# Attention and two MLP layers on one core: a third load queue and a re-ordered start

## The chip, the cores and the metric

The kernel runs on one core of one Trainium2 chip. The metric is the device time of one execution in microseconds (us), the median of several runs; a part of the text speaks of one profiled execution, whose instructions were recorded. A change of under 0.2% (2.08 us) is about what a measurement of this kernel can't tell from no change.

## What is computed

```python
def _attn_ref(q, k, v, tau):                      # q, k, v: 1 x 6016 x 256
    qn = q / (norm(q, axis=1) + 1e-06)            # one norm per column, over all 6016 rows
    kn = k / (norm(k, axis=1) + 1e-06)
    s = kn.T @ qn / tau                           # 256 x 256
    a = softmax(s, axis=-1)
    return v @ a

x = v @ a                                         # 6016 x 256
x = gelu_sigmoid(x @ w_in) @ w_out                # hidden size 2048
x = leaky_relu(x @ w2_in) @ w2_out
```

The inputs are 32-bit floats (the weights come as 64-bit words that the kernel converts).

## The kernel before

**Front.** q and k are read once. A block is 128 rows of q and the same 128 rows of k, 256 KB together. `rows` (L327) says how many blocks each load tile has: six tiles of one, one of two, nine of four, then one of two and one of one, 47 blocks in all. Eight buffers hold tiles; `load_qk(j)` (L335) issues one transfer for q and one for k, from SyncE's queue (SP), except that the k of tiles 0 to 3 goes out from ScalarE's queue. `AHEAD = 8` tiles are issued before the loop, and each turn of the loop (L392) issues the tile eight further on, after the scores and squares of its own tile.

For each block TensorE adds 128 rows of k against 128 rows of q into two score banks (`scores`, L360). A 256-column product of plain 32-bit floats runs as two instructions, so a block costs four. From tile `LATE` on (15 blocks) only the first score half is done in the loop, and the second halves are kept as reserve work for later (`second_half`, L510). ScalarE squares q and k two blocks at a time and VectorE adds the squares into `acc`, which has two halves (one per block of the pair; `squares`, L352). When all tiles are through, L411 adds the second half of `acc` to the first, and `norms` (L372) sums the rows with four one-column products against `ones`, eight instructions in all. From their result VectorE and ScalarE make the inverse norms, then come the softmax halves (L457), and while these run TensorE transposes v and works off the reserve.

**Order of conversion work.** The weights are converted in the gaps of VectorE by a generator, `jobs` (L294): each `go_on(n)` lets the next n steps be issued. A piece of the first weight (`wi`) has five steps: a shift (L212), two word operations (L217, L221), a copy that is the high half (L240), and a subtraction that is the low half (through L99). Pieces of the second weight (`wo`) have the same three and then L233 and a subtraction. At the third step the next piece's load is issued on SP, and `scale_next` lets ScalarE scale the next piece (L182), unless the list `held` is filled.

**The step to the layers.** The softmax matrix is multiplied into `w_in` (`fold_products`, L485): `fold(f)` (L572) makes the weights of hidden part f from the converted piece wi of f, whose high half its first two products read and whose low half the next two. The first pair of row blocks goes through `hidden_first` (L746): for f = 0, each of two column halves u is multiplied, activated on ScalarE, split into high and low halves (`halves`, L94: ScalarE casts, VectorE subtracts) and then one conversion step is let through; for other f the split is done for both u at once with four conversion steps before the subtraction. All later products go through `terms` (L88):

```python
for w, x, start, stop in ((wh, ah, first, False), (wh, al, False, False), (wl, ah, False, last)):
```

Every product of 32-bit accuracy is thus three: high by high, high weight by low data, low weight by high data. Each engine executes its own queue strictly in the order written.

Of the kernel before, what the change touches and what calls it, by code (L numbers as in the profile page):

```python
# [17 lines left out]
def tile_kernel(  # L18
# [28 lines left out]
    nc = tc.nc  # L47
    _, N, C = q.shape
    F = w_out.shape[0]
    P = 128  # L50
    KC = C // P
    NF = F // P // 2
# [21 lines left out]
    ident = const.tile([P, P], F32, name="ident")  # L74

    def small(pool, n, name):
        return pool.tile([P, 32], F32, name=name)[:, :n]

    ones = const.tile([P, P], F32, name="ones")
# [5 lines left out]
    def bank(tag):  # L85
        return ps.tile([P, BLK], F32, tag=tag, name=tag)

    def terms(dst, ws, xs, first, last, more=False):  # L88

        (wh, wl), (ah, al) = ws, xs  # L90
        for w, x, start, stop in ((wh, ah, first, False), (wh, al, False, False), (wl, ah, False, last)):
            nc.tensor.matmul(dst, lhsT=w, rhs=x, start=start, stop=stop, skip_group_check=more)  # L92

    def halves(hi, lo, raw):  # L94
        nc.scalar.copy(hi, raw)  # L95
        nc.vector.tensor_tensor(out=lo, in0=raw, in1=hi.bitcast(F32), op=ALU.subtract)  # L96

    def add(out, in0, in1, op=ALU.add):
        nc.vector.tensor_tensor(out=out, in0=in0, in1=in1, op=op)  # L99

    def subtract(out, in0, in1):
        add(out, in0, in1, ALU.subtract)
# [11 lines left out]
    with tc.manual_schedule():  # L114
# [14 lines left out]
        etl = early.tile([P, KC, C], F32R, tag="tt", name="etl")  # L129

        nc.gpsimd.memset(ones, 1.0)
        make_identity(nc, ident)


        raws = {}
# [28 lines left out]
        def next_load():  # L164
            if to_load and len(raws) < 3:
                load_piece(to_load.pop(0))
# [12 lines left out]
        def scale_words(t):  # L179

            h = t[:, :, :, 1].bitcast(F32)
            nc.scalar.activation(out=h, in_=h, func=AF.Copy, scale=2.0 ** -112)  # L182
# [3 lines left out]
        held = [True]  # L186
# [6 lines left out]
        def scale_next():  # L193
            if held:
                return
            for key in to_convert[:2]:
                if key in raws and key not in scaled:
                    scale_words(raws[key])
                    scaled.add(key)
                    return  # L200
# [104 lines left out]
        def go_on(count):  # L305
            for _ in range(count):
                next(work, None)
# [3 lines left out]
        acc = front.tile([P, 2, 2, C], F32, name="acc")  # L311
# [4 lines left out]
        root, rr, rn = (small(front, 4, x) for x in ("root", "rr", "rn"))  # L316
# [7 lines left out]
        nc.vector.memset(acc, 0.0)  # L324


        rows = [1] * 6 + [2] + [4] * 9 + [2, 1]  # L327
        assert sum(rows) * P == N
        at = [sum(rows[:j]) * P for j in range(len(rows))]
        last = len(rows) - 1  # L330

        def qk(j):
            return big[(j // 2 + 2) % 4][:, j % 2]

        def load_qk(j):  # L335
            n = rows[j]
            for i, src in ((0, q), (1, k)):
                eng = nc.scalar if j < 4 and i == 1 else nc.sync
                eng.dma_start(  # L339
                    out=qk(j)[:, i, :n, :],  # L340
                    in_=src[at[j]:at[j] + n * P, :].rearrange("(p r) c -> p r c", r=n),
                )
# [1 line left out]


        AHEAD = 8
        V_TILE = 10
        LATE = last - 4
        s_ps = [bank("y00"), bank("y10")]
        nrm = bank("h0")  # L350

        def squares(j):  # L352
            t, n = qk(j), rows[j]
            for r in range(0, n, 2):
                m = min(2, n - r)
                sq = front.tile([P, 2, 2, C], F32, tag="sq", name="sq", bufs=3)[:, :, :m]
                nc.scalar.activation(out=sq, in_=t[:, :, r:r + m, :], func=AF.Square)  # L357
                add(acc[:, :, :m, :], acc[:, :, :m, :], sq)
# [12 lines left out]

        def norms():  # L372

            for i in range(2):
                for kc in range(KC):
                    nc.tensor.matmul(  # L376
                        nrm[:, 2 * i + kc:2 * i + kc + 1],
                        lhsT=acc[:, i, 0, kc * P:(kc + 1) * P],
                        rhs=ones[:, :1],
                        start=True,  # L380
                        stop=True,
                    )

        for j in range(AHEAD):
            load_qk(j)
            if j == 3:
                nc.scalar.preload_act_table(AF.Sqrt)

        warm = bank("h3")
        for _ in range(6):  # L390
            nc.tensor.matmul(warm[:, :P], lhsT=ones, rhs=ones, start=True, stop=True)
        for j in range(LATE + 1):  # L392
# [3 lines left out]
            if j + AHEAD <= last:  # L396
                load_qk(j + AHEAD)
            if j == V_TILE:
                next_load()
                nc.sync.dma_start(out=taub, in_=tau.partition_broadcast(P))  # L400
                for c in range(2):
                    nc.sync.dma_start(
                        out=qk(V_TILE)[:, c],
                        in_=v[c * BLK:(c + 1) * BLK, :].rearrange("(t p) c -> p t c", p=P),
# [3 lines left out]

        for j in range(LATE + 1, last + 1):
            squares(j)  # L410
        add(acc[:, :, 0, :], acc[:, :, 0, :], acc[:, :, 1, :])  # L411
        for j in range(LATE + 1, last + 1):
            scores(j, (0,))
        go_on(2)
        norms()

        nc.vector.reciprocal(out=rtau, in_=taub)
        nc.vector.tensor_scalar_add(rr, nrm[:, :4], 1e-35)
        nc.scalar.activation(out=root, in_=rr, func=AF.Sqrt)
        nc.vector.reciprocal(out=rn, in_=root)  # L420
        nc.vector.tensor_tensor(out=rr, in0=rr, in1=rn, op=ALU.mult)
# [22 lines left out]
        def transpose_v(kc, tags):  # L444
            for u, tag in enumerate(tags):
                vt[kc, u] = bank(tag)
                for i in range(BLK // P):
                    nc.tensor.transpose(  # L448
                        vt[kc, u][:, i * P:(i + 1) * P],
                        qk(V_TILE)[:, u, i, kc * P:(kc + 1) * P], ident,  # L450
                    )

        def split_v(kc, u):
            dst = xbt if kc else xa[0]
            halves(dst[:, 0, u], dst[:, 1, u], vt[kc, u])
# [39 lines left out]
        def fold_scale(raw, pw, kc):  # L495
            nc.scalar.activation(  # L496
                out=raw[:, 0::3] if kc == 0 else raw[:, 1:3],
                in_=pw.rearrange("p (s n) -> p s n", s=2), func=AF.Copy,
                scale=rden[:, kc:kc + 1],
            )  # L500
# [61 lines left out]
        fold_scale(raw0, pw0[1], 1)  # L562
        fold_half(raw0, 0, 1)
        nc.sync.dma_start(out=w1raw[0], in_=raw0)
        go_on(1)
        split_v(1, 1)
        nc.scalar.preload_act_table(AF.Gelu_apprx_sigmoid)
        first_products(0, [(0, 1), (1, 1)])
        held.clear()
        go_on(3)  # L570

        def fold(f):  # L572

            wi = ready.pop(f)
            pw = bank("h0" if f == 1 else "h3").rearrange("p (k n) -> p k n", k=KC)
            for kc in range(KC):
                fold_products(pw[:, kc], wi, kc)
            raw = early.tile([P, 4, P], F32, tag="tp", name="raw")
            for kc in range(KC):
                fold_scale(raw, pw[:, kc], kc)  # L580
            hi, lo = wa[f][:, 0, :4], wa[f][:, 1, :4]
            nc.vector.tensor_copy(hi, raw)
            subtract(lo, raw, hi.bitcast(F32))
            nc.sync.dma_start(out=w1raw[f], in_=raw)
# [161 lines left out]
        def hidden_first(f):  # L746

            s, g = f // NF, f % NF
            at = (A11, A12) if s == 0 else (A21, A22)
            h = late.tile([P, 2, BLK], F32, tag="cc", name="h")  # L750
            gd = late.tile([P, 2, 2, BLK], F32R, tag="gd", name="gd", bufs=2)
            for u in range(2):
                if g == 0:
                    hp = hp0[s, u]
                    first_products(1, [(s, u)])
                else:
                    hp = bank(f"h{2 * s + u}")
                    for kc, x in enumerate((xa[0], xbt)):
                        terms(hp, (wa[g][:, 0, at[kc]], wa[g][:, 1, at[kc]]),
                              (x[:, 0, u], x[:, 1, u]), kc == 0, kc == KC - 1)  # L760
                act(1, h[:, u], hp)
                if g == 0:
                    halves(gd[:, 0, u], gd[:, 1, u], h[:, u])
                    go_on(1)
            if g:
                nc.scalar.copy(gd[:, 0], h)
                if f < 2 * NF - 1:
                    go_on(4)
                subtract(gd[:, 1], h, gd[:, 0].bitcast(F32))
            for u in range(2):  # L770
                pend.append((1, 0, u, f, gd[:, 0, u], gd[:, 1, u]))
# [6 lines left out]
        for f in range(NF):  # L778
            for s in range(2):
                hidden_first(f + s * NF)  # L780

                if f + 1 < NF and s == 0 and f:
                    while f + 1 not in ready:
                        go_on(1)
                    fold(f + 1)
                if f == 0 and s == 0:
                    continue
                if f == 0:
                    while 1 not in ready:
                        go_on(1)  # L790
                    emit_y(1)
                    fold(1)
                    emit_y(3)
                    fetch()
                else:
                    emit_y(len(pend) - 2)
                if f + 1 < NF or s == 0:
                    go_on(2)
                fetch()
# [180 lines left out]
```

## Time and profile before

| | |
|---|---|
| median of 3 runs | 1040.09 us (1039.96 to 1041.32) |
| the profiled execution's own time | 1040.84 us |
| its span, first to last instruction | 1039.1 us |
| TensorE (PE) busy | 1029.1 us, 99% |
| VectorE (DVE) busy | 774.8 us, 75% |
| ScalarE (ACT) busy | 592.5 us, 57% |
| GpSimd (POOL) busy | 0.8 us |
| mean granted TensorE clock | 1.000 of full |

The profile names a group of instructions by line, engine, operation, and output <- inputs. In the timeline the columns are start, length, engine, line, operation, how many, and in brackets how long the engine had been idle before and what released it. Successive matmuls overlap, so the length of one is longer than the distance to the next. "PEld" is the weight load of TensorE, "SPq" and "ACTq" a queue's issue of transfers.

### The profile page before, as it was taken

The page shows a single profiled execution, that of the slowest core. Times are in us where ns is not written, and L with a number is a line of the kernel's source. Part 1 is how long each engine was busy: PE and PEld are TensorE (multiplying, and loading weights), DVE is VectorE, ACT ScalarE, POOL GpSimd, SP SyncE. Part 2 cuts the span into 40 slices and gives each one's busy share as a digit, 9 for nine tenths or more (in the row PEclk, how much of TensorE's full clock was granted, in tenths as well). Part 3 has the DMA queues.
Part 4 walks back from the last instruction along what each step waited for, and adds up shares of the span by engine and source line. Part 5 has one row for each costly group of instructions (what it writes and reads, how often), then busy time and mean ns, then how long its engine had stood idle before and what let it go on. Part 6 is the DMA issues. An engine that isn't in the chain of part 4 may idle for free.

```text
span 1039.1 us, 12654 instructions
## 1 busy us (share of the span) xinstructions
PE 1029.1 (99%) x4670; PEld 868.0 (84%) x4670; DVE 774.8 (75%) x1195; ACT 592.5 (57%) x880; POOL 0.8 (0%) x7
## 2 busy tenths in 40 slices
PE   8999999999999999999999999999999999999998
PEld 7878888888888888888998888888888888888997
DVE  6889968888888888888866667667577667676655
ACT  5665556565666666665656555555555555455453
POOL 0000000000000000000000000000000000000000
PEclk9999999999999999999999999999999999999999
DMA  8745324014224223222744002001200300300202
GB/s 327 270 132 145 119 82 94 18 31 122 81 72 124 79 71 120 79 95 104 258 168 152 1 1 46 37 1 22 60 0 10 72 1 1 77 1 1 41 1 36
DMA packets 120941, 81.82 MB, mean 79 GB/s; under 512 B 93488, under 2 KB 105520, under 8 KB 119600
## 3 DMA queue, kind: packets, MB, share of 16 engines
q1 hardware_dynamic: 116592, 80.04, 25.6%
q10 hardware_dynamic: 4288, 0.98, 0.4%
q8 instruction: 36, 0.59, 0.2%
q14 instruction: 25, 0.20, 0.1%
HBM read 55.05 MB, written 25.95 MB: 78 GB/s over the span
## 4 chain that ended last, share of the span: by engine, by line
PE 95%; DMA 2%; DVE 2%; ACT 1%; issue 0%; ACTq 0%; SPq 0%; DVEq 0%
PE y L92 49%; PE h L92 43%; DMA qk<-in_k_dram 2%; DVE acc L99 1%; PE h L491 1%; PE y L364 1%; ACT sq L357 0%; ACT cv L182 0%; DVE xb L96 0%; PE h L376 0%; PE h L448 0%; ACTq L339 0%; PE y L448 0%; ACT raw L496 0%; PE y L491 0%
## 5 line engine op out<-in xcount | busy, mean ns | idle before, releaser
L92 PE MATMUL y<-gd,wo 128*128 128x512 f32 (+1 forms) x1248 | 296.9, 386 | 0.1
L92 PE MATMUL h<-xa,wa 128*128 128x512 f32 (+1 forms) x1152 | 276.2, 385 | 0.2 <-ACT raw L496 0.2
L92 PEld LDWEIGHTS y<-gd,wo 128*128 128x128 f32 x1248 | 233.7, 188 | 44.7 <-DVE gd L96 0.5
L92 PEld LDWEIGHTS h<-xa,wa 128*128 128x128 f32 x1152 | 215.9, 188 | 40.7 <-ACT raw L496 0.7
L92 PE MATMUL y<-g,wo 128*128 128x512 f32 (+1 forms) x1044 | 246.8, 385 | 0.0
L92 PEld LDWEIGHTS y<-g,wo 128*128 128x128 f32 x1044 | 196.0, 188 | 36.3
L92 PE MATMUL h<-xb,wa 128*128 128x512 f32 (+1 forms) x888 | 217.2, 385 | 0.4 <-DVE xb L96 0.4
L92 PEld LDWEIGHTS h<-xb,wa 128*128 128x128 f32 x888 | 166.6, 188 | 31.9 <-DVE xb L96 0.8
L99 DVE TENSOR_TENSOR tv<-tp,h 128x512 f32<-128x512 f32 (+1 forms) x88 | 59.3, 674 | 113.2 <-PE h L92 108.1
L99 DVE TENSOR_TENSOR cc<-tv,h 128x512 f32<-128x512 f32 (+1 forms) x176 | 116.0, 673 | 35.7 <-PE h L92 35.3
L96 DVE TENSOR_TENSOR gd<-cc,gd 128x1024 fp32r<-128x1024 f32 (+1 forms) x87 | 104.0, 1196 | 0.0
L817 ACT COPY tp<-h 128x512 f32<-128x512 f32 (+1 forms) x87 | 50.4, 579 | 91.8 <-PE h L92 90.1
L95 ACT CAST gd<-cc 128x1024 fp32r<-128x1024 f32 (+1 forms) x87 | 90.0, 1034 | 0.0
L596 ACT ACTIVATE cc<-cc 128x1024 f32<-128x1024 f32 (+2 forms) x49 | 50.3, 1027 | 38.8 <-DVE cc L99 38.8
L596 ACT ACTIVATE tt<-tt 128x512 f32<-128x512 f32 (+1 forms) x48 | 30.0, 625 | 72.5 <-DVE tt L99 72.5
L99 DVE TENSOR_TENSOR tt<-tt,h 128x512 f32<-128x512 f32 (+1 forms) x88 | 59.5, 676 | 9.5 <-DVE tt L99 0.5
L99 DVE TENSOR_TENSOR tt<-tv,h 128x512 f32<-128x512 f32 (+1 forms) x88 | 59.5, 676 | 9.2
L594 ACT ACTIVATE cc<-cc 128x1024 f32<-128x1024 f32 (+1 forms) x40 | 41.6, 1040 | 41.2 <-DVE cc L99 41.2
L99 DVE TENSOR_TENSOR g<-tt,g 128x512 fp32r<-128x512 f32 (+1 forms) x87 | 58.5, 673 | 7.2 <-ACT g L828 7.0
L594 ACT ACTIVATE tt<-tt 128x512 f32<-128x512 f32 (+1 forms) x40 | 24.9, 623 | 62.4 <-DVE tt L99 62.4
L99 DVE TENSOR_TENSOR g<-tp,g 128x512 fp32r<-128x512 f32 (+1 forms) x87 | 58.6, 673 | 0.0
L841 ACT CAST g<-tp 128x512 fp32r<-128x512 f32 (+1 forms) x87 | 53.3, 612 | 2.8
(111 smaller groups left out, 705.6 us busy)
## 6 DMA issues: line engine op xcount, KB each, us to landing
cv<-in_moe_w_in_dram SPq DMA_DIRECT2D x32, 256.0 KB, 3.3
cv<-in_moe_w_out_dram SPq DMA_DIRECT2D x16, 512.0 KB, 3.7
wa<-w2a SPq DMA_DIRECT2D x8, 896.0 KB, 4.6
x<-stg SPq DMA_DIRECT2D x5, 1024.0 KB, 4.3
stg<-x SPq DMA_DIRECT2D x5, 1024.0 KB, 5.1
out_dram<-o SPq DMA_DIRECT2D x80, 64.0 KB, 1.9
qk<-in_q_dram SPq DMA_DIRECT2D x9, 512.0 KB, 10.2
qk<-in_k_dram SPq DMA_DIRECT2D x9, 512.0 KB, 10.7
```

The source lines that it names most:

```text
L92: nc.tensor.matmul(dst, lhsT=w, rhs=x, start=start, stop=stop, skip_group_check=more)
L95: nc.scalar.copy(hi, raw)
L96: nc.vector.tensor_tensor(out=lo, in0=raw, in1=hi.bitcast(F32), op=ALU.subtract)
L99: nc.vector.tensor_tensor(out=out, in0=in0, in1=in1, op=op)
L364: nc.tensor.matmul(s_ps[h][:, :C], lhsT=t[:, 1, r, h * P:(h + 1) * P], rhs=t[:, 0, r, :], start=(j == 0 and r == 0), stop=(j == last and r ...
L491: nc.tensor.matmul(pw, lhsT=e[:, d, c0], rhs=wi[:, x, d], start=i == 0, stop=i == len(todo) - 1)
L594: nc.scalar.activation(out=out, in_=in_, func=AF.Gelu_apprx_sigmoid)
L596: nc.scalar.activation(out=out, in_=in_, func=AF.Prelu, alpha=0.01)
L817: nc.scalar.copy(tp, pa)
L841: nc.scalar.copy(g11[:, 0], tp)
```

## The change

The change does the following.

- **Load tiles.** `rows` becomes four tiles of one block, ten of four, one of two and one of one. The tiles 4 and 5 (four blocks each) are issued from GpSimd's queue, q and k both: four transfers of 512 KB. The k of tiles 0 to 3 stays on ScalarE's queue, all else on SP. `V_TILE`, the loop turn that loads v and the first weights, goes from 10 to 8. `make_identity`, GpSimd work, moves behind the first eight tiles' loads.
- **Norms.** The addition of the halves of `acc` goes. `norms` sums both halves by eight one-column products, the second half first, and a four-column addition on VectorE joins the two sums.
- **Products.** `terms` takes the low half of the data last, after the low half of the weight.
- **Conversion steps.** A `go_on(1)` ahead of `split_v(1, 1)` goes. `held` is cleared not ahead of the first hidden part but after its second column half. At f = 1 (first s) `held` is filled again, six steps are let through in place of four, and `held` is cleared after the `fold` that follows.

```diff
-        for w, x, start, stop in ((wh, ah, first, False), (wh, al, False, False), (wl, ah, False, last)):
+        for w, x, start, stop in ((wh, ah, first, False), (wl, ah, False, False), (wh, al, False, last)):
...
-        make_identity(nc, ident)
...
-        rows = [1] * 6 + [2] + [4] * 9 + [2, 1]
+        rows = [1] * 4 + [4] * 10 + [2, 1]
...
-                eng = nc.scalar if j < 4 and i == 1 else nc.sync
+                eng = nc.gpsimd if j in (4, 5) else nc.scalar if j < 4 and i == 1 else nc.sync
...
-        V_TILE = 10
+        V_TILE = 8
...
-            for i in range(2):
-                for kc in range(KC):
-                    nc.tensor.matmul(
-                        nrm[:, 2 * i + kc:2 * i + kc + 1],
-                        lhsT=acc[:, i, 0, kc * P:(kc + 1) * P],
+            for m in (1, 0):
+                for i in range(2):
+                    for kc in range(KC):
+                        col = 4 * m + 2 * i + kc
+                        nc.tensor.matmul(
+                            nrm[:, col:col + 1],
+                            lhsT=acc[:, i, m, kc * P:(kc + 1) * P],
...
         for j in range(AHEAD):
             load_qk(j)
             if j == 3:
                 nc.scalar.preload_act_table(AF.Sqrt)
+        make_identity(nc, ident)
...
-        add(acc[:, :, 0, :], acc[:, :, 0, :], acc[:, :, 1, :])
...
-        nc.vector.tensor_scalar_add(rr, nrm[:, :4], 1e-35)
+        nc.vector.tensor_scalar_add(rr, nrm[:, 4:8], 1e-35)
+        add(rr, rr, nrm[:, :4])
...
-        go_on(1)
         split_v(1, 1)
...
         first_products(0, [(0, 1), (1, 1)])
-        held.clear()
         go_on(3)
...
                     halves(gd[:, 0, u], gd[:, 1, u], h[:, u])
+                    if f == 0 and u == 1:
+                        held.clear()
+                        scale_next()
                     go_on(1)
...
-                if f < 2 * NF - 1:
+                if f == 1:
+                    held.append(True)
+                    go_on(6)
+                elif f < 2 * NF - 1:
                     go_on(4)
...
                     fold(f + 1)
+                    if held:
+                        held.clear()
+                        scale_next()
```

## Rows read from the trace of the kernel before

**Rows 1.** Busy time by stretch: us, each engine's busy (instructions), PEclk, DMA share, GB/s.

```profile
0.00:15.00 15.00, 10.97 (x46) 9.07 (x47) 6.29 (x8) 6.34 (x9) 0.84 (x7) 1.00 0.80 263
...
80.00:130.00 50.00, 50.00 (x245) 42.31 (x244) 46.62 (x76) 28.49 (x46) 0.00 (x0) 1.00 0.43 132
```

**Rows 2.** Timeline of TensorE, 9 to 28 us: the score products.

```profile
11.06 1.97 PE L364 MATMUL y<-qk 128*128 128x256 f32 x8 [1.28 <-DMA qk<-in_k_dram]
14.67 13.62 PE L364 MATMUL y<-qk 128*128 128x256 f32 x62 [1.64 <-DMA qk<-in_k_dram]
```

**Rows 3.** Timeline of SyncE's queue in short windows: issues of q.

```profile
0.73 1.83 SPq L339 DMA_DIRECT2D qk<-in_q_dram  x4
...
3.58 0.33 SPq L339 DMA_DIRECT2D qk<-in_q_dram  x1
...
6.88 0.43 SPq L339 DMA_DIRECT2D qk<-in_q_dram  x1
...
13.32 0.33 SPq L339 DMA_DIRECT2D qk<-in_q_dram  x1
```

**Rows 4.** Transfers issued from 0.7 and from 6.8 us: size, us to landing.

```profile
qk<-in_q_dram SPq DMA_DIRECT2D x1, 128.0 KB, 2.6
...
qk<-in_q_dram SPq DMA_DIRECT2D x1, 512.0 KB, 6.4
```

**Rows 5.** Busy time by stretch, 0 to 15 us: the last column is GB/s.

```profile
0.00:4.00 4.00, 3.01 (x13) 3.01 (x14) 0.91 (x1) 1.35 (x2) 0.84 (x7) 1.00 0.53 154
4.00:8.00 4.00, 3.89 (x17) 3.06 (x17) 2.58 (x4) 2.94 (x6) 0.00 (x0) 1.00 0.91 283
8.00:12.00 4.00, 2.72 (x14) 2.08 (x12) 1.57 (x3) 1.60 (x2) 0.00 (x0) 1.00 0.84 262
12.00:15.00 3.00, 1.36 (x7) 0.91 (x6) 1.23 (x1) 0.45 (x2) 0.00 (x0) 1.00 0.99 384
```

**Rows 6.** Timeline, 39 to 60 us: last scores, the added halves, the norms.

```profile
38.70 3.40 PE L364 MATMUL y<-qk 128*128 128x256 f32 x15
...
42.24 0.69 DVE L99 TENSOR_TENSOR acc<-acc 128x512 f32<-128x512 f32 x1
...
42.99 1.05 PE L376 MATMUL h<-ones,acc 128*128 128x1 f32 x8 [0.89 <-DVE acc L99]
```

**Rows 7.** Timeline of VectorE, 57 to 65 us: splits and conversion steps.

```profile
58.02 0.68 DVE L96 TENSOR_TENSOR xb<-y,xb 128x512 fp32r<-128x512 f32 x1
...
61.01 0.42 DVE L240 CAST wi<-ta 128x512 fp32r<-128x512 f32 x1
61.40 0.69 DVE L96 TENSOR_TENSOR gd<-h,gd 128x512 fp32r<-128x512 f32 x1
62.01 0.68 DVE L99 TENSOR_TENSOR wi<-ta,wi 128x512 fp32r<-128x512 f32 x1
63.47 0.69 DVE L96 TENSOR_TENSOR gd<-h,gd 128x512 fp32r<-128x512 f32 x1 [0.78 <-ACT gd L95]
```

**Rows 8.** Timeline of TensorE and ScalarE, 57 to 65 us: first hidden part, fold of f = 1.

```profile
58.76 2.10 PE L92 MATMUL h<-xb,wa 128*128 128x512 f32 x8 [0.36 <-DVE xb L96]
...
62.19 0.60 ACT L594 ACTIVATE h<-h 128x512 f32<-128x512 f32 x1 [0.82 <-DVE gd L96]
...
62.41 0.84 PE L491 MATMUL h<-wi,eth 128*128 128x256 f32 x4
...
64.05 1.32 PE L92 MATMUL y<-gd,wo 128*128 128x512 f32 x5
```

**Rows 9.** Timeline of TensorE and ScalarE, 72.3 to 75.7 us: after the fold of f = 2.

```profile
72.31 0.86 PE L92 MATMUL h<-xa,wa 128*128 128x512 f32 x3
73.00 0.85 PE L92 MATMUL h<-xb,wa 128*128 128x512 f32 x3
74.10 0.96 PE L92 MATMUL h<-xa,wa 128*128 128x512 f32 x3 [0.24 <-ACT raw L496]
...
72.66 0.68 ACT L182 ACTIVATE cv<-cv 128x512 f32<-128x512 f32 x1
```

More of the change, by code (lines that the diff above doesn't have):

```diff
@@ L372, in norms @@
         def norms():
-            for i in range(2):
-                for kc in range(KC):
-                    nc.tensor.matmul(
-                        nrm[:, 2 * i + kc:2 * i + kc + 1],
-                        lhsT=acc[:, i, 0, kc * P:(kc + 1) * P],
[L379 to L382, printed above, removed]
+            for m in (1, 0):
[5 more added lines that the diff above has]
+                            lhsT=acc[:, i, m, kc * P:(kc + 1) * P],
+                            rhs=ones[:, :1],
+                            start=True,
+                            stop=True,
+                        )
         for j in range(AHEAD):
```

## The prediction, made before the changed kernel ran

> **What bounds the kernel now.** The page comes first: TensorE is busy for 1029.1 of 1039.1 us, so whatever the change does elsewhere, the time moves only where TensorE waits or where it gets more to do. The busy time by stretch says where that is: in the first 15 us TensorE is busy for 10.97, and from 80 us on the stretch is full, 50.00 of 50.00, at the full clock [rows 1]; the later stretches look the same, up to the last output. So at most some 10 us are to be had, and those that this change touches lie before 80 us. I read that part in order of time, with the timeline.
>
> *Data.* After the six one-block tiles TensorE waits 1.28 us for the two-block tile and, when that is done, 1.64 us for the first tile of four [rows 2]: 2.92 us together. From 14.67 us on it never waits for q and k again; 62 matmuls in 13.62 us are 0.22 us each, 0.88 for a block.
>
> *Issue.* SP issues four q in its first 1.83 us, but the next only at 3.58 [rows 3]. The first q, out at 0.73, landed 2.6 us later, at 3.33 [rows 4]. In the same way the 512 KB out at 6.88 land 6.4 us later, at 13.28, and an issue follows at 13.32, with seven others out in between. So a transfer of SP and ScalarE goes out when the one eight before it is in: that, not SP's own work, holds the early loads back.
>
> *Rate.* Up to 12 us the DMA engines move 154, 283 and 262 GB/s, and 384 in the next 3 us [rows 5]. Summed up that is 0.62 MB by 4 us, 1.75 by 8, 2.80 by 12 and 3.95 by 15.
>
> *Norms.* TensorE's scores end at 42.10 (38.70 + 3.40), VectorE's last square is added when the addition of the halves begins, at 42.24, and TensorE waits 0.89 us for that addition before the norms [rows 6].
>
> *Conversions.* From 57 to 75 us there are small waits: for the low half of xb, for that of wi, for ScalarE's fold scaling [rows 7 to 9].
>
> **The change part by part.**
>
> *Load tiles.* Twelve blocks stood before TensorE's last wait was over in the old order: eight in the first seven tiles, four in the next. In the new order the same twelve are tiles 0 to 5, and 12 x 0.262 MB = 3.15 MB must be in before TensorE can run through. By the rates, 3.15 MB had moved at 12.92 us (12 + 0.35 / 0.384), and the tile was usable at 14.67, 1.75 us later. The GpSimd issues don't occur in this trace, so I bound them. Best: both waits go, -2.92 us. Worst: the bytes come at the old rate, but GpSimd's two tiles share the engines with tiles 6 and 7 from SP, which follow q 3 closely. At an equal share for half of that time 1.05 MB of the later tiles come in between, tile 5 needs 4.2 MB, which is 15.66 us by the rates and 17.4 with the same 1.75: +2.7 us. Between: as many bytes by the same time in the right order, so that TensorE has done eight blocks and gets the next four at 14.67 as now. I take that, **0**, because the rows show the engines moving data nearly without a break from 4 us on (share 0.91 and 0.84), and an earlier issue doesn't make bytes move faster by itself. Both ends stay for the range. The number of blocks before LATE (32), the 15 in the tail and the block after which v is loaded (24) are as before, so nothing changes behind. make_identity waits behind four issues on GpSimd; its result is first read by the transposes behind the norms, some 40 us later, so it costs nothing unless an issue hangs that long. SP's q of tile 6 moves up past the four transfers that left its queue.
>
> The skill has a rule that would make it come out otherwise. The Trainium skill, "DMA: Bandwidth & Descriptors", section "Queues, rings and completion order", says that each DMA engine takes turns between the queues that have work for it, a packet at a time. No row here shows three queues at once; by that rule the load term is the +2.7 of the worst case and not 0, and it is the mechanism of the first rival.
>
> *Norms.* Four more one-column products are eight more instructions, 1.05 us by the row of the present eight. The second half of acc is complete one addition before the end, so they can begin when the scores end, 42.10, and run to 43.15; the first half's follow to 44.20. Now the norms end at 42.99 + 1.05 = 44.04 [rows 6]. So **+0.16**: a wait of 0.89 is filled with 1.05 of work. VectorE's 0.69 goes, but it isn't what ends last any more. The extra four-column addition lies under transposes and reserve scores, where TensorE has work of its own; if that cover went it would cost one short operation.
>
> *Low data last.* The number of products is the same and each loads its weights as before; from 80 us on TensorE doesn't wait, so nothing is won there: **0**. Before that it gives VectorE one product more for the low half of data and takes one from the low half of weights.
>
> *The step left out and held.* VectorE now splits xb 0.60 us earlier (the low half of wo steps behind it), and ScalarE does the scaling of a piece after both column halves of the first hidden part and not ahead of the first. That takes away the 0.36 that TensorE waits for xb [rows 8]. But every conversion step of this stretch now comes one place later, and the first that is late is the low half of wi for f = 1. Now the order on VectorE is high half of wi (61.01), gd of the second column half (61.40), low half of wi (62.01, done 62.69), and then an idle stretch until gd of the next part (63.47) [rows 7]. In the new order the high half of wi slides behind gd: gd starts 0.39 earlier, at 61.01. ScalarE's next activation, which waits for just that gd as h has one buffer [rows 8], starts at 61.80 in place of 62.19; the gd that hangs on it, 1.28 us after, at 63.08. The low half of wi now stands behind this gd, since one go_on(1) less has been spent: 0.61 later, at 63.69, done at 64.37 and not at 62.69. The fold's third product reads it. TensorE began the fold at 62.41 and went on to 64.05 [rows 8], with the low half as its bound in both cases, so the fold ends 64.37 - 62.69 = **+1.68** later, and what was gained for xb only makes TensorE wait longer there. Behind TensorE's fold stand 18 products that are ready; they wait with it. A VectorE that overtakes (if the wait for ScalarE is shorter than now) would bring this down to 0.
>
> *Held at f = 1.* The matmuls that follow the fold of f = 2 need the bank that ScalarE's fold scaling empties, and ScalarE first scales a weight piece for 0.68. Without it TensorE would go on one step (73.00 - 72.31 = 0.69) after 73.00, at 73.69, not 74.10 [rows 9]: **-0.41**. Six steps in place of four fill a stretch in which VectorE waits for ScalarE, and bring it back to its old place in the conversions.
>
> Sum: 0 + 0.16 + 0 + 1.68 - 0.41 = +1.43 us. On the profiled execution's 1040.84 (a span of 1039.1 and 1.7 around it) that is 1042.27; that execution was 0.75 above the median, and on the median it is 1041.5.
>
> **The rivals.**
>
> *Slower: the queues take turns.* Tile 5 comes after half of tiles 6 and 7, at 17.4 us. For it: SP's queue has tile 6 ready to go at 3.33, when the first q is in, long before 2 MB can have moved. Against it: GpSimd begins earlier, and its descriptors may be ahead in each engine. The price is +2.7 on top, 1040.09 + 1.43 + 2.7 = 1044.2. A milder form is that one-block tiles 1 to 3 wait behind GpSimd's 4 KB rows. It decides for slower as soon as tile 5 is usable after 15.3 us (2.08 - 1.43 = 0.65 after 14.67).
>
> *Faster: the data waits go.* If more transfers under way lift the rate of the first 12 us to the 384 GB/s seen behind, tiles 4 and 5 come before TensorE wants them, -2.92. For it: the low rate goes with the time in which transfers are held back. Against it: the engines' share is already 0.8 to 0.9 there. With 0.16 - 0.41, and the fold's wait at 0 to 1.68, it is -3.2 to -1.5, or 1036.9 to 1038.6.
>
> *The low half of wi isn't late* and the data come as now: 0.16 - 0.41 = -0.25, 1039.8. It needs VectorE to reach it before gd, against the written order.
>
> *The third queue isn't one:* if GpSimd's transfers are counted among the same eight, they leave at 3.33 or later, as tiles 4 and 5 do now. The load term is then the 0 of the forecast.
>
> **How the numbers follow.** The forecast (with the last rival inside) has 0.34, turns between queues 0.32, the data waits gone 0.24, wi in time 0.10. The likeliest gives 1041.5, own range 1040.0 to 1042.6. Faster by over 0.2% (under 1038.0; about what a measurement of this kernel tells from no change) is most of the third: 0.22. Slower by over 0.2% (above 1042.2) is the second and the forecast's upper edge: 0.34. Within 0.2%: 0.44. The range goes from between the ends of the fast rival, 1037.3, to the slow one's 1044.2.
>
> **What would show it.** Right: TensorE's last wait for q and k ends near 14.7 us; no wait between the scores and the norms, which take 2.1 us; the fold of f = 1 waits for the low half of wi for over a microsecond; no wait after the fold of f = 2. Wrong: a rate above 350 GB/s before 10 us (the fast rival), a landing of tile 5 beyond 15.3 us or a late tile 1 (the slow one), or a wi low half that is done before the second gd.

## The result and the profile after

The changed kernel takes 1046.78 us in the median of 5 runs (1044.94 to 1047.67), the kernel before 1040.33 beside it: a ratio of 1.006 with a 95% interval of 1.0048 to 1.0072. It is slower, and by more than the range allowed (1044.2). The profiled execution was the fastest of the five, 1044.94 us with a span of 1043.0.

TensorE's last product starts at 1037.19 us and not at 1033.88, so of the 4.10 us between the two profiled executions +3.31 lie ahead of it. From its start to the end of the span it is 5.8 us and not 5.2: the change and the four kernels below with both its tiles and GpSimd's queue all have 5.8, the others 5.2 to 5.5, and why isn't shown. The medians differ by 2.35 us more than the profiled executions, and that part stands in no trace. I divide the 3.31 at two marks: the end of the scores, and the start of the transposes of v behind the norms. The scores end at 44.51 in place of 42.10 (+2.41); from there to the transposes it is 1.54 us in place of 1.80 (-0.26); from there to the last product 991.14 in place of 989.98 (+1.16).

TensorE's timeline of the changed kernel, from the first scores to the transposes of v. The waits of [rows 2] and [rows 6] are answered by these lines:

```profile
3.73 2.19 PE L363 MATMUL y<-qk 128*128 128x256 f32 x8
8.68 1.13 PE L363 MATMUL y<-qk 128*128 128x256 f32 x4 [2.76 <-DMA qk<-in_k_dram]
11.04 5.19 PE L363 MATMUL y<-qk 128*128 128x256 f32 x15 [1.23 <-DMA qk<-in_k_dram]
...
41.76 2.75 PE L363 MATMUL y<-qk 128*128 128x256 f32 x12
44.34 1.84 PE L377 MATMUL h<-ones,acc 128*128 128x1 f32 x16
46.05 1.07 PE L450 MATMUL h<-ident,qk 128*128 128x128 f32 x8
```

After two tiles TensorE waits 2.76 us for tile 2 and then 1.23 for tile 3, both tiles of one block. It never waits for tiles 4 and 5. The products behind the second wait are slow: 15 in 5.19 us, where 62 took 13.62 before. The busy time by stretch tells why; the columns are those of [rows 5], with PEclk, the granted clock, third from the end:

```profile
6.00:8.00 2.00, 0.00 (x0) 0.00 (x0) 0.09 (x1) 0.00 (x0) 0.00 (x0) 1.00 1.02 366
8.00:10.00 2.00, 1.13 (x4) 0.68 (x4) 0.68 (x1) 0.63 (x1) 0.00 (x0) 1.00 1.05 410
10.00:12.00 2.00, 0.96 (x3) 0.78 (x4) 0.28 (x2) 0.93 (x2) 0.00 (x0) 0.79 1.03 421
12.00:14.00 2.00, 2.00 (x6) 1.64 (x5) 1.65 (x2) 1.60 (x2) 0.00 (x0) 0.50 1.02 414
14.00:16.00 2.00, 2.00 (x9) 1.67 (x9) 1.89 (x2) 1.88 (x2) 0.00 (x0) 0.86 1.03 414
```

After those two waits the granted clock is 0.50, the 1.2 GHz level, and six products stand in 2 us, where stretches at the full 2.4 GHz have eleven (keep_busy below shows two). From 6 us on the engines move 366 to 421 GB/s, more than the 283 and 262 of before [rows 5]. So bytes came faster, and the wrong ones came first. The transfers by queue, from 4 to 6 and from 6 to 8 us (q0 is GpSimd's queue, q1 SP's, q10 ScalarE's; packets, MB, share of the engines' time):

```profile
q0 software_dynamic: 128, 0.46, 58.0%
q1 hardware_dynamic: 64, 0.07, 17.4%
q10 hardware_dynamic: 31, 0.03, 6.6%
...
q0 software_dynamic: 123, 0.47, 61.8%
q10 hardware_dynamic: 142, 0.13, 20.6%
q1 hardware_dynamic: 143, 0.13, 20.0%
```

From 6 to 8 us the three queues have nearly the same number of packets, but GpSimd's are 4 KB and the others 1 KB: 0.47 MB go to tiles that nobody wants yet and 0.26 to the two that TensorE waits for. From 4 to 6 us it is more uneven, 0.46 MB against 0.10, and GpSimd's queue has more packets than the other two together. Equal turns don't explain that stretch, and no run here does. The q of tile 3, issued in the window from 2.1 us, needs 7.8 us to land; its like needed 4.3 before (the second line, the median of two):

```profile
qk<-in_q_dram SPq DMA_DIRECT2D x1, 128.0 KB, 7.8
...
qk<-in_q_dram SPq DMA_DIRECT2D x2, 128.0 KB, 4.3
```

Behind the norms, VectorE's steps that answer to [rows 7], and then TensorE's products that answer to [rows 8] and [rows 9], both from the timeline of the changed kernel:

```profile
63.05 0.69 DVE L96 TENSOR_TENSOR gd<-h,gd 128x512 fp32r<-128x512 f32 x1
63.65 0.42 DVE L239 CAST wi<-ta 128x512 fp32r<-128x512 f32 x1
65.11 0.69 DVE L96 TENSOR_TENSOR gd<-h,gd 128x512 fp32r<-128x512 f32 x1 [1.04 <-ACT gd L95]
65.72 0.69 DVE L99 TENSOR_TENSOR wi<-ta,wi 128x512 fp32r<-128x512 f32 x1
```

```profile
64.12 0.50 PE L493 MATMUL h<-wi,eth 128*128 128x256 f32 x2 [0.27 <-DVE wi L239]
66.46 0.50 PE L493 MATMUL h<-wi,eth 128*128 128x256 f32 x2 [1.83 <-DVE wi L99]
...
67.75 4.27 PE L92 MATMUL y<-gd,wo 128*128 128x512 f32 x18
...
77.41 0.85 PE L92 MATMUL h<-xa,wa 128*128 128x512 f32 x3
```

VectorE stands idle for 1.04 us until ScalarE has the next gd, with the low half of wi in its queue behind it, and TensorE waits 1.83 us for that half. The products behind the fold start at 67.75, and those that had waited for ScalarE's scaling [rows 9] at 77.41, now without a wait.

The five runs differ with the clock: mean granted 0.998 and 0.997 at 1044.94 and 1045.64 us, 0.994 at 1046.78, 1047.51 and 1047.67. Only the first was recorded instruction by instruction.

### The profile page after: what moved, and what is told of

Its sections match the earlier page's. It is cut to its first block, busy times and chain, and to the rows that moved or that the text cites. A ratio compares the mean times of both kernels' runs of the same rounds, so it can differ in the third digit from the quotient of the medians.

```text
span 1043.0 us, 12673 instructions
## 1 busy us (share of the span) xinstructions
PE 1030.6 (99%) x4678; PEld 870.2 (83%) x4678; DVE 774.6 (74%) x1194; ACT 593.8 (57%) x879; POOL 3.2 (0%) x11
## 4 chain that ended last, share of the span: by engine, by line
PE 97%; DMA 1%; DVE 0%; ACT 0%; ACTq 0%; issue 0%; SPq 0%
PE y L92 49%; PE h L92 43%; PE y L363 4%; DMA qk<-in_k_dram 1%; PE h L493 1%; DMA cv<-in_moe_w_in_dram 0%; DVE gd L96 0%; ACT h L594 0%; PE h L377 0%; PE y L493 0%; ACTq L338 0%; ACT L568 0%; ACT gd L95 0%; PE h L450 0%; PE y L450 0%; DVE wo L99 0%
## 5 line engine op out<-in xcount | busy, mean ns | idle before, releaser
L594 ACT ACTIVATE cc<-cc 128x1024 f32<-128x1024 f32 (+1 forms) x40 | 41.7, 1042 | 42.4 <-DVE cc L99 42.4
```

What stands on the lines that cost most here:

```text
L594: nc.scalar.activation(out=out, in_=in_, func=AF.Gelu_apprx_sigmoid)
```

## The experiments

Medians, with the kernel before run on the same chip; the last column is the range of the mean granted clock over a kernel's runs. The kernel before had 0.997 to 1.000 itself, with runs from 1039.19 to 1043.01 us. My theory was that GpSimd's rows hold up the one-block tiles, that the waits for these bring the clock down, and that the fold's wait comes from VectorE's order; the rivals stand with each expectation.

| kernel | us | before beside it | ratio, 95% interval | clock |
|---|---|---|---|---|
| the change | 1046.78 | 1040.33 | 1.0048 to 1.0072 | 0.994 to 0.998 |
| old_loads | 1042.77 | 1040.44 | 1.0008 to 1.003 | 0.996 to 1.000 |
| new_loads | 1043.52 | 1040.44 | 1.0016 to 1.0037 | 0.996 to 0.997 |
| keep_busy | 1043.62 | 1040.44 | 1.0022 to 1.0041 | 0.997 to 0.999 |
| fold_early | 1044.7 | 1040.44 | 1.002 to 1.0046 | 0.995 to 0.997 |
| sp_only | 1039.79 | 1040.0 | 0.9986 to 1.0006 | 0.998 to 1.000 |
| pool_small | 1038.52 | 1040.0 | 0.9979 to 0.9998 | 0.998 to 1.000 |
| both_mended | 1042.26 | 1040.0 | 1.0011 to 1.0029 | 0.999 to 1.000 |
| old_loads_fold | 1039.9 | 1040.0 | 0.9991 to 1.001 | 0.998 to 1.000 |
| small_all | 1038.24 | 1040.27 | 0.997 to 0.9988 | 0.999 to 1.000 |
| small_old_terms | 1037.96 | 1040.27 | 0.9968 to 0.9986 | 0.999 to 1.000 |

### The load tiles alone, and all but the load tiles

The first kernel is the change without its load tiles:

```diff
-        rows = [1] * 4 + [4] * 10 + [2, 1]
+        rows = [1] * 6 + [2] + [4] * 9 + [2, 1]
...
-                eng = nc.gpsimd if j in (4, 5) else nc.scalar if j < 4 and i == 1 else nc.sync
+                eng = nc.scalar if j < 4 and i == 1 else nc.sync
...
-        V_TILE = 8
+        V_TILE = 10
```

> The changed kernel with the load tiles of before (six tiles of one block, no transfer from GpSimd, v at turn 10); norms, product order and conversion steps stay changed. Theory (the third queue delays the one-block tiles, and the waits bring TensorE's clock down): no wait above 1.7 us for q and k, clock 1.000, norms about 0.2 us later than in the kernel before, the fold of f = 1 still some 1.6 late: 1041.3 to 1042, that is 1 to 1.5 us over before and 5 under the change. Rival (the loss comes from the norms and the conversion steps): still over 1044.

The second is the kernel before with these lines the other way round, and `make_identity` behind the loads.

> The kernel before with nothing but the new load tiles, GpSimd's queue, the moved identity and v at turn 8. Theory: tiles 2 and 3 usable near 8.7 and 11 us as in the changed kernel, clock below 1.000, scores done 2 to 5 us later: 1042.5 to 1045.5. Rival (the loads give time, the other parts lose it): 1040 or less.

The load tiles alone cost 3.1 us (1043.52 against 1040.44), all else 2.3, and 5.4 together against the 6.45 of the change. So the theory holds for the loads: their trace has the two waits again (1.64 and 1.47 us), the clock falls to 0.50 behind them, and the scores end at 46.24 (43.70 + 2.54):

```profile
12.00:14.00 2.00, 2.00 (x6) 1.55 (x6) 1.45 (x2) 2.00 (x3) 0.00 (x0) 0.50 1.01 406
14.00:16.00 2.00, 2.00 (x6) 1.58 (x5) 1.69 (x2) 0.45 (x2) 0.00 (x0) 0.50 1.04 416
...
43.70 2.54 PE L363 MATMUL y<-qk 128*128 128x256 f32 x11
```

The waits are shorter than in the change's profile, where TensorE came to the first of them sooner: the eight products ahead of it took 3.64 us here and 2.19 there. But the low clock lasts longer: what a wait costs isn't its length alone. Without the load tiles more was left than I had expected (1041.3 to 1042, at a clock of 1.000). The stretch from the transposes to the last product is 991.13 us there, as in the change; its recorded execution was among the fastest of its ten (1040.98), and the others ran at 0.996 to 1.000.

### TensorE kept at work in the two waits

```diff
+            for _ in range((0, 0, 10, 5)[j] if j < 4 else 0):
+                nc.tensor.matmul(warm[:, :P], lhsT=ones, rhs=ones, start=True, stop=True)
             scores(j, range(KC) if j < LATE else (0,))
```

> The changed kernel with 10 and 5 additional products of ones by ones (128 columns, no use of their result) ahead of the scores of tiles 2 and 3, where TensorE waits. Theory (the clock drops because TensorE stands idle there): granted clock 1.000 from 11 to 15 us, scores done 1 to 1.5 us sooner than in the changed kernel's profile, and all runs alike, 1043 to 1044. Rival (the clock falls for another reason): half clock after 11 us as before, and runs from 1045 to 1048.

The profile is as the theory has it: the data come nearly as late as in the change (ScalarE's first squares of tiles 2 and 3 start at 8.24 and 10.61 us, in the change at 8.66 and 11.07), but the clock stays at 1.00, eleven instructions go through in 2 us where there were six, and the scores end at 42.37 (37.67 + 4.70), 2.1 us sooner.

```profile
12.00:14.00 2.00, 2.00 (x11) 1.77 (x10) 1.68 (x2) 1.13 (x2) 0.00 (x0) 1.00 1.04 422
14.00:16.00 2.00, 2.00 (x11) 1.77 (x10) 1.08 (x2) 1.40 (x2) 0.00 (x0) 1.00 1.01 404
```

Of that, 0.46 is a tile 3 that landed sooner (its scores begin at 10.58 and not at 11.04). So the clock fell because TensorE stood idle there, and beside the waits themselves, 3.99 us, the low clock cost some 1.7. That all runs would be alike was a miss: they go from 1042.66 to 1045.2. One wait of 1.8 us was left in this kernel, that for wi.

### The low half of wi sooner

```diff
+                if f == NF and u == 0:
+                    go_on(1)
                 if g == 0:
                     halves(gd[:, 0, u], gd[:, 1, u], h[:, u])
...
-                    go_on(1)
+                    if f != NF or u:
+                        go_on(1)
```

> The changed kernel with one conversion step of the second hidden part moved ahead of the first split there, so that VectorE makes the low half of wi while it waits for ScalarE. Theory (the fold of f = 1 waits for that half): the wait of 1.83 us there falls below 0.4, and the time by 1.3 to 1.7 us against the change at the same clock. Rival (another wait takes its place): less than 0.5.

The wait for the low half is 0.22 in place of 1.83:

```profile
67.32 0.50 PE L493 MATMUL h<-wi,eth 128*128 128x256 f32 x2 [0.22 <-DVE wi L99]
```

From the transposes to the last product it is 989.56 us (48.52 to 1038.08), 1.58 less than in the change and 0.42 less than in the kernel before. The median is 2.1 below that of the change (measured in another set of runs, whose kernel before is 0.1 higher), in spite of longer data waits in its recorded run (3.71 and 1.56 us). The step was the one foreseen, and no other wait took its place.

### Both mended

The two edits together: the data come late, but TensorE has no long wait.

> The changed kernel with the additional products ahead of tiles 2 and 3 and the conversion step moved ahead, so that TensorE has no wait of over 0.5 us left before 80 us. Theory (what differs from run to run is the clock after a wait; in the kernel with additional products alone the fold's wait was left): clock 0.999 or more in all runs, spread under 1 us, 1041 to 1042. Rival (the spread has another source): runs again from 1042 to 1045.

All ten runs lie from 1041.8 to 1042.61, with a clock of 0.999 or 1.000. One data wait of 0.95 us was left, and the median lies 0.3 us over what was expected. With the wait for wi (keep_busy) the runs spread over 2.5 us, without it over 0.8. That supports the clock as the source of the spread; at which place it fell in the runs that were not recorded isn't shown.

### Which part of the loads: the queue or the tile sizes

In sp_only the tiles are the change's, but no transfer goes through GpSimd; in pool_small the tiles are those of before, and GpSimd's queue has tiles 4 and 5, of one block. Both are otherwise the kernel before, with `make_identity` behind the loads.

```diff
# sp_only
-        rows = [1] * 6 + [2] + [4] * 9 + [2, 1]
+        rows = [1] * 4 + [4] * 10 + [2, 1]
...
-        V_TILE = 10
+        V_TILE = 8
# pool_small
-                eng = nc.scalar if j < 4 and i == 1 else nc.sync
+                eng = nc.gpsimd if j in (4, 5) else nc.scalar if j < 4 and i == 1 else nc.sync
```

> The kernel before with the new load tiles (four of one block, ten of four, v at turn 8), all transfers but the first four k from SyncE's queue, none from GpSimd. Theory (GpSimd's 4 KB rows take turns with the 1 KB rows, packet for packet): tiles 2 and 3 land near 5 and 6.5 us as in the kernel before and TensorE does not wait for them; it waits once, some 3 us, for tile 4. Scores done about as before; 1040 to 1042.5. Rival (the larger tiles delay tiles 2 and 3, whatever queue they are on): waits for tile 2 and 3 as in the change, 1043 or more.

> The kernel before with its own tiles of one block, but tiles 4 and 5 (1 KB rows like tiles 0 to 3) from GpSimd's queue, and the identity moved. Theory (rows of one size share fairly, and four more transfers under way lift the rate): the one-block tiles land without a wait, over 330 GB/s before 10 us, the waits for q and k fall from 2.9 to under 1.5 us, norms 1 to 2.5 us sooner, clock 1.000: 1038 to 1039.5. Rival (GpSimd's queue itself is what delays): waits as in the change, over 1042.

TensorE's waits for q and k, first of sp_only and then of pool_small:

```profile
6.20 1.99 PE L363 MATMUL y<-qk 128*128 128x256 f32 x8 [0.46 <-DMA qk<-in_k_dram]
10.16 10.13 PE L363 MATMUL y<-qk 128*128 128x256 f32 x38 [1.96 <-DMA qk<-in_k_dram]
```

```profile
7.70 12.57 PE L363 MATMUL y<-qk 128*128 128x256 f32 x57 [0.80 <-DMA qk<-in_k_dram]
```

With the same tile sizes on SP, tile 2 is there at 6.20 and not at 8.68, and the loss is gone (1039.79 against 1040.0), although the clock falls to 0.50 from 12 to 14 us here too, behind the second wait. (I had expected no wait for tile 2.) So the sizes alone don't cost, and the third queue alone doesn't either: in pool_small the median is 1.5 us below before. What costs is the two together.

That the third queue wins here because all early rows have one size, as I expected, isn't borne out by the trace. First GpSimd's queue over the whole run of pool_small, then this queue and ScalarE's from 4 to 6 us:

```profile
q0 software_dynamic: 192, 0.52, 0.2%
...
q0 software_dynamic: 51, 0.13, 22.3%
q10 hardware_dynamic: 128, 0.12, 19.2%
```

The rows that GpSimd loads are 1 KB, but 0.52 MB in rows of 1 KB would be 512 packets, and they came in 192: its queue moves larger packets beside those of 1 KB here too. What differs from new_loads is the amount, 0.52 MB in place of 2.10. So larger packets beside smaller ones weren't enough for a loss; together with 2.10 MB that nobody wanted yet they were. The large amount in packets of 1 KB wasn't tried, so what the packet size does by itself stays open.

In the recorded executions the data waits fall from 2.92 to 0.80 us, and the transposes begin at 42.08 and not at 43.90. A part of that is the spread between executions: small_all and small_old_terms, below, have the same loads and wait 0.75 and 2.24 us, and old_loads and old_loads_fold, with the loads of before, 1.11 and 1.82. The end of the scores tells more: it lies at 40.0 to 40.8 us in the three kernels with pool_small's loads and at 41.2 to 42.1 in the three with those of before. The engines move 376 GB/s from 6 to 8 us and 413 from 8 to 10. Not as expected: tile 2 is late here too, as six tiles now share the engines, and the rate has a hole from 4 to 6 us (199 GB/s).

### What is good of the rest

> The change without its load tiles and queue and with the conversion step moved ahead. Theory: against the same kernel without that step (1042.77) the fold's wait of 1.8 us goes, and with it runs at a lower clock: 1039.3 to 1040.5, at or a little below the kernel before. Rival (norms, product order and held cost something themselves): 1041.5 or more.

This is old_loads with the step of fold_early. It is 1039.9 against 1040.0, so norms, product order and `held` cost nothing together once the fold's wait is gone; in the trace they gain (scores' end to transposes 1.54, then 989.57 to the last product, 0.41 less than before).

The next kernel adds pool_small's queue to it, the last one has the product order of before besides.

> The changed kernel with the tiles of before, where GpSimd's queue loads tiles 4 and 5 of one block (so all early rows are 1 KB), and with the conversion step moved ahead: everything of the change that theory holds for good. From the earlier runs: the front of the kernel with small tiles from GpSimd (transposes of v from 42.1 us, or a little sooner, since the norms don't wait for the added halves) and the stretch behind it of the kernels with the moved step (989.6 us to TensorE's last product): 1037.5 to 1038.3, 2 below before. Rival (the gains overlap): not below the 1038.5 of small tiles alone.

> The kernel of the run beside it with the product order of before (low half of the data second). Theory (after 80 us TensorE never waits, and before that the order matters only at the first hidden part): 0.2 to 0.8 us slower, in the waits between 59 and 63 us alone; from 80 us on the same. Rival (the order matters throughout): over 2 us slower.

The first is 2.0 us faster than before, 1038.24, at the upper edge of what was expected; that it also beats pool_small is not settled (0.3 us, from different sets of runs). The second misses its expectation: 1037.96, not slower at all. From the transposes to the last product it needs 989.33 us and the kernel beside it 989.58. Behind the norms and before 80 us TensorE has three small waits in small_all, in the other one:

```profile
PE h L493 <- DVE wi L239: 0.3, 1, 0.3
PE y L92 <- DVE wo L99: 0.3, 1, 0.3
PE h L493 <- DVE wi L99: 0.2, 1, 0.2
```

```profile
PE h L493 <- DVE wi L99: 0.2, 1, 0.2
```

The new order needs wo's low half one product sooner, and waits 0.3 us for it; it wins nothing that the traces show. The last kernel is the fastest tried: 2.3 us or 0.22% under before, 8.8 under the change on medians from two sets of runs.

## Why the prediction was wrong

**The load term was 0 and measured +2.41.** The step that failed is "as many bytes by the same time in the right order". More bytes came (366 to 421 GB/s where the rows gave 262 to 283), in the wrong order; the reason given, that an earlier issue doesn't make bytes move faster by itself, didn't hold. I had the mechanism as a rival and put its damage at the wrong place: I priced a late tile 5, and gave half a sentence to "one-block tiles 1 to 3 wait behind GpSimd's 4 KB rows", without a price. By that sentence the sum could be done: in a turn of three packets two of 1 KB stand against one of 4 KB, so the small tiles get a third of the bytes. The packets by queue show such a turn from 6 to 8 us, 123, 142 and 143; from 4 to 6 us the small tiles got less still, 0.10 of 0.56 MB. The Trainium skill ("DMA: Bandwidth & Descriptors", "Queues, rings and completion order") says that each DMA engine takes turns between the queues that have work for it, a packet at a time. The trace agrees by its equal counts from 6 to 8 us and not by those from 4 to 6, and how many rows make a turn it doesn't show. The rival should have had more weight than my 0. Its +2.7 lies near the +2.41 by luck: it is the price of a late tile 5, and TensorE never waited for that.

**The clock was not in the sum at all.** The rows before show a granted clock of 1.00 [rows 1], [rows 5], and I took it as given. Of the 2.41 us, 1.07 are longer waits (3.99 against 2.92); the rest, some 1.3, lies in the products. The lower level behind the waits cost some 1.7, and some 0.4 came back ahead of them: before, the 24 products up to the first wait took 6.07 us, 0.8 more than at 0.22 each, and in the change the eight took 2.19, 0.4 more.

```profile
3.71 6.07 PE L364 MATMUL y<-qk 128*128 128x256 f32 x24
```

keep_busy shows that this isn't the data's fault: same tiles, same queue, clock 1.00, and 1.7 us sooner than tile 3's landing explains. The median lies 1.84 us over the profiled run, at a lower mean clock; that the clock is all of these 1.84 isn't shown.

**Norms:** +0.16 predicted, -0.26 measured. The mis-sized term is the eight further instructions: sixteen take 1.84 us, so the second eight cost 0.79 and not 1.05, and the first starts 0.17 us ahead of the modelled end of the scores (44.34 against 44.51). That the wait of 0.89 goes was right.

**The low half of wi:** +1.68 predicted; the fold ends 21.70 us after the transposes begin (46.05 to 67.75) in place of 20.15, so +1.55. The wait is where the order of VectorE's queue put it, and fold_early takes it away by the order alone. The walk through the queue was right. In the medians the removal was worth more, 2.4 us from old_loads to old_loads_fold, each against the kernel before beside it; the clock (0.996 to 1.000 without it, 0.998 to 1.000 with it) may be the difference, which isn't shown.

**Held at f = 1:** -0.41 predicted. From the end of the fold of f = 1 to the products that had waited for ScalarE's scaling it is 9.66 us (67.75 to 77.41) in place of 10.05: -0.39, as predicted, though no run has this part by itself.

**Low data last:** 0 predicted, and 0.25 us worse in the trace of small_all than in that of small_old_terms; in the medians nothing to be told.

So the parts that could be walked through in the rows came within 0.5 us each, and the error that the traces show is one term that the rows before didn't have, together with a second cost that hangs on it. The slow rival had the sign. "The third queue isn't one" fell: GpSimd's four issues go out from 1.28 us, 0.53 to 0.67 each, without waiting for a landing.

## What to carry to other kernels

A further queue makes transfers start sooner, but they share the engines with what is wanted first: here 0.52 MB on the third queue gained and 2.10 MB lost. What is wanted first should have little beside it, or stand ahead of the rest in one queue; look at the packets and MB by queue, since a queue's packets need not be the rows as written. A wait on TensorE near the start is worth more than its length when the clock falls behind it; look at the granted clock behind each wait, and give TensorE something to do there if the wait can't go. When conversion steps are shifted by one in a hand-written order, look for the step that slides behind an instruction with a wait of its own.

## What was not expected of the hardware

Two waits of 2.76 and 1.23 us, with four products between them, took the clock from 1.00 to 0.50, while single waits of 1.28 and 1.64 us before, with eight products between, left it at 1.00. A single one of 2.24 in small_old_terms left it there too. In new_loads the clock fell behind 1.64 and 1.47 with four products between, and it stayed low longer than behind the longer waits; in sp_only it fell behind 0.46 and 1.96 with eight between. How long it stays down varies from run to run; by what it is set remains open.

In the first microseconds a granted clock of 1.00 is no evidence. In the change's trace the clock's records begin 4.3 us into the span and in that of new_loads 7.2, and ahead of its records a stretch reads 1.00. Before, the 12 warm-up instructions of 128 columns took 2.93 us in such a stretch, while in keep_busy 20 like them took 2.40 from 6.36 us on; the eight score instructions of the first two tiles took 2.19 us in the change and 3.64 in new_loads. There the distance between products tells the pace. The lines of before, keep_busy and new_loads:

```profile
0.99 2.93 PE L391 MATMUL h<-ones 128*128 128x128 f32 x12 [0.99 <-POOL ones L131]
...
6.36 2.40 PE L396 MATMUL h<-ones 128*128 128x128 f32 x20
...
3.72 3.64 PE L363 MATMUL y<-qk 128*128 128x256 f32 x8
```

The low transfer rate from 4 to 12 us, 262 to 283 GB/s, is not fixed: with the very same loads old_loads has 330 from 8 to 10 us, with larger early tiles it was 359 from 6 to 8 us on the same two queues (sp_only), with a third queue 366 to 376. Whether it hangs on the bytes under way or on the number of issues was not separated.
